# Linear attention, RMS norm and a leaky-ReLU feed-forward on one core: alternating the output's PSUM banks, holding two output products, and pinning ScalarE instructions

## The chip, the core and the metric

The kernel runs on one core of a Trainium2 chip. Its engines are TensorE (PE in the profile; PEld is its weight load), VectorE (DVE), ScalarE (ACT), GpSimd (POOL) and SyncE (SP), which work side by side and wait for each other through semaphores. TensorE writes its results to PSUM, which has banks; VectorE and ScalarE read them out ("drain" them) from there. The metric is the device time of one execution in microseconds; lower is better.

## What is computed

Eight batches of eight heads go through linear attention with an RMS norm, the result is read as 4608 tokens of width 512, and these go through a feed-forward block with 2048 hidden units. All is fp32.

```python
# q, k, v: (8, 8, 576, 64)
kv  = einsum('bhsd,bhse->bhde', k, v)
out = einsum('bhsd,bhde->bhse', q, kv)
rms = sqrt(mean(out * out, axis=-1, keepdims=True) + 1e-06)
x   = (out / rms * g_norm)            # -> transposed and reshaped to (4608, 512)
h   = x @ w_in                        # (4608, 2048)
g   = maximum(0.01 * h, h)
y   = g @ w_out                       # (4608, 512)
```

## The kernel before

The 4608 tokens are 9 blocks (NB) of 512. Block 0 is done with plain matmuls while attention and weights are still being prepared (`first_block`). Blocks 1 to 8 use Strassen's scheme: a product of 2 by 2 matrices in seven smaller products with sums around them. The hidden units are cut into four chunks (NC) per block, so a block has 4 x 7 = 28 slots. In each slot TensorE does one of the seven hidden products of a chunk (from block 2 on, two levels of Strassen) and then one of the seven output products of an earlier chunk, two slots behind (LAG).

The seven products are taken in the order 1, 2, 6, 5, 7, 3, 4. Products 1, 6, 7, 4 add up in one PSUM bank (tag 0 below) and 2, 5, 3 in the other (tag 1). Each product is read out by `done` before its bank can be written again.

```python
ORDER = (1, 2, 6, 5, 7, 3, 4)
FRESH = (1, 2, 5)

def strassen(tags, left, right, done):
    banks = {}
    for i in ORDER:
        b = tags[0 if i in (1, 6, 7, 4) else 1]
        if i in FRESH:
            banks[b] = ps_m.tile([P, 2, N2], F32, tag=b, name=f"{b[0]}_{b[1]}")   # one buffer per tag
        bank = banks[b]
        for part in range(2):
            for r in range(2):
                matmul(bank[:, part, :], lhsT=left(i, part, r), rhs=right(i, part, r), ...)
        done(i, bank.rearrange("p u (v n) -> p (u v) n", v=2))
        yield
```

The output product of chunk n (n counts chunks over the blocks 1 to 8). `to` is the sum in SBUF; only in a block's first chunk is a fresh product copied by ScalarE, everything else is a VectorE add.

```python
def product_o(n, g_sides, os, finish):
    c = n % NC
    w_sides, _ = sides_w2(n)
    sums = sides_w2(n + 1)[1] if n + 1 < NC * (NB - 1) else lambda i: None   # next chunk's weight sums by DMA
    ...
    def done(i, bank):
        key, fresh = into[i]
        to = os[key].rearrange("p u (v n) -> p (u v) n", v=2)
        if c == 0 and fresh:
            nc.scalar.copy(to, bank)
        else:
            add(nc.vector, to, bank, to)
        if c == NC - 1 and i in (2, 7, 3, 4):
            finish(key, os[key])                      # store to DRAM
        if i == 5:   sums(0)
        elif i == 4: sums(1)

    yield from strassen(("oa", "oc") if n + 1 < NC * (NB - 1) else ("hd", "hc"), ...)
```

The hidden chunk's end: sums on VectorE, four leaky ReLUs on ScalarE, four sums on GpSimd, of which output products 5, 6, 7 and 3 take s1, s2, s3 and s4.

```python
    # product_h_two, after the seven products
    add(nc.vector, g21, qa[:, :, 0, :], qa[:, :, 1, :])
    add(nc.vector, g11, qa[:, :, 0, :], qc[:, :, 0, :])
    yield
    add(nc.vector, g22, g21, qa[:, :, 2, :])
    add(nc.vector, g12, g22, qa[:, :, 3, :])
    yield
    add(nc.vector, g22, g22, qc[:, :, 1, :])
    add(nc.vector, g21, g21, qc[:, :, 1, :])
    add(nc.vector, g21, g21, qc[:, :, 2, :])
    for t in (g11, g12, g22, g21):
        relu(t)                                       # ScalarE
    sums_of(c, to):
        s1 = g21 + g22;  s2 = s1 - g11;  s3 = g11 - g21;  s4 = g12 - s2      # GpSimd
```

The division by the root mean square in `divide`, on VectorE and ScalarE by turns (the last root of a tile is one small ScalarE instruction between two VectorE ones):

```python
    for l in range(2):
        t = t2k(n, "turned")
        in_turn(nc.vector.transpose(t, sums[l]))
        in_turn(nc.vector.tensor_reduce(rms[:, l, :], t..., op=ALU.add))
        if l:
            nc.scalar.activation(rms, rms, func=AF.Sqrt, scale=1.0 / D, bias=eps_sb)
        yield
    in_turn(nc.vector.reciprocal(rms, rms))
    for l in range(2):
        nc.scalar.copy(spread..., rms[:, l, :] broadcast)
    ...
```

The last lines of block 0's loop: each hidden tile is activated by ScalarE and then multiplied by the second weight.

```python
    for n in range(2 * NC * U + 1):
        now = last
        if n < 2 * NC * U:
            ...matmuls into h_ps...
            gT = view(g_all[n // 4 % 2], n % 4 * NT, NT)
            nc.scalar.activation(gT, h_ps, func=AF.Prelu, alpha=SLOPE)
            last = (gT, w2_sb[h][c][:, u, :], n)
        ...
        for t in range(4):
            matmul(accs[t], lhsT=now[0][:, t * P:(t + 1) * P], rhs=now[1], ...)
```

The main loop, cut to what drives the output products:

```python
    for i in range(1, NB):
        ...
        for c in range(NC):
            ...
            for t in range(7):
                slot = 7 * c + t
                go(h_steps, 1)          # one hidden product
                ...                     # attention and sums for later blocks, in given slots
                if waited == LAG:
                    go_o()              # one output product
                elif o_queue:
                    waited += 1
                ...
            if i == NB - 1 and c == NC - 1:
                go(h_steps, 1)
                go_o()
            go(h_steps)
            ...
            o_queue.append(product_o((i - 1) * NC + c, g_sides, os, store(i)))
    while go_o():
        pass
```

The order of instructions on an engine is set when the program is built: a scheduler puts them in an order of its own from dependencies and its estimates of time, except where an instruction is pinned. `pin` ties an instruction behind the one that was written before it for the same engine. All matmuls are pinned, and from block 2 on (`steady`) the VectorE instructions too; most of ScalarE's are not.

Of the kernel before, what the change touches and what calls it, by code (L numbers as in the profile page):

```python
# [12 lines left out]
AF = mybir.ActivationFunctionType  # L13
# [10 lines left out]
def kernel(  # L24
# [36 lines left out]
    nc = tc.nc  # L61
    B, H, S, D = q.shape
# [8 lines left out]
    NB = B * S // NT  # L71
    N2 = NT // 2
    U = 2
    NC = DF // 2 // (U * P)
    SLOPE = 0.01
# [12 lines left out]
    ps_m = ctx.enter_context(tc.tile_pool(name="ps_m", bufs=1, space=bass.MemoryType.PSUM))  # L88

    pin = tc.keep_in_program_order  # L90
    steady = False

    def in_turn(ins):

        if steady:
            pin(ins)
# [188 lines left out]
    eps_sb = consts.tile([P, 1], F32, name="eps_sb")  # L285
# [44 lines left out]
    def x_of(lo, hi):  # L330
        return block(lo // NT)[:, :, lo % NT:lo % NT + hi - lo]
# [25 lines left out]
    def divide(lo, hi, sums):  # L357

        x, n = x_of(lo, hi), hi - lo
        rms = work.tile([P, 2, n // E], F32, tag="rms", name="rms", bufs=2)  # L360
# [3 lines that stand above are left out]
            in_turn(nc.vector.tensor_reduce(rms[:, l, :], t.rearrange("p (a i) -> p a i", i=E),  # L364
                                            axis=AX.X, op=ALU.add))
            if l:
                nc.scalar.activation(rms, rms, func=AF.Sqrt, scale=1.0 / D, bias=eps_sb)
            yield
        in_turn(nc.vector.reciprocal(rms, rms))
        spread = []  # L370
        for l in range(2):
            t = t2k(n, "spread")
            nc.scalar.copy(t.rearrange("p (a i) -> p a i", i=E),
                           rms[:, l, :].unsqueeze(2).to_broadcast([P, n // E, E]))
            spread.append(t)
        yield
        for l in range(2):
            inv = t2k(n, "inv")
            in_turn(nc.vector.transpose(inv, spread[l]))
            to = x[:, 2 * l:2 * l + 2, :]  # L380
            in_turn(nc.vector.tensor_mul(to, to, inv.unsqueeze(1).to_broadcast([P, 2, n])))
            yield
# [458 lines left out]
# [3 lines that stand above are left out]
        sums = sides_w2(n + 1)[1] if n + 1 < NC * (NB - 1) else lambda i: None  # L844
        if c == 0:
            for key in ("11", "12", "21", "22"):
                os[key] = opool.tile([P, 2, N2], F32, tag="o", name=f"o{key}", bufs=6)

        into = {1: ("11", True), 5: ("22", True), 2: ("11", False), 6: ("12", True),
                3: ("12", False), 7: ("22", False), 4: ("21", True)}  # L850
# [9 lines that stand above are left out]
                finish(key, os[key])  # L860

            if i == 5:
                sums(0)
            elif i == 4:
                sums(1)


        yield from strassen(("oa", "oc") if n + 1 < NC * (NB - 1) else ("hd", "hc"), lambda i, part, r: g_sides[i][:, 2 * r + part, :],
                            lambda i, part, r: w_sides[i][:, r, :], done)

    def go(steps, n=None):
# [13 lines left out]
    def first_block(between):  # L885

        accs = [ps_m.tile([P, DM], F32, tag=t, name="o_acc") for t in ("oa", "oc", "hb", "hd")]
        x, last = xTs.pop(0), None
# [3 lines that stand above are left out]
                c, h, u = n // (2 * U), n // U % 2, n % U  # L892
                h_ps = ps_m.tile([P, NT], F32, tag=("ha", "hc")[n % 2], name="h_ps")

                parts = 2 if n == 0 else 1
                for part in range(parts):
                    cols = slice(part * NT // parts, (part + 1) * NT // parts)
                    for e in range(NE):
                        matmul(h_ps[:, cols], lhsT=w1_sb[h][c][:, u, e, :],
                               rhs=x[:, e, cols], start=(e == 0 and part == 0),  # L900
                               stop=(e == NE - 1), skip_group_check=True)
                gT = view(g_all[n // 4 % 2], n % 4 * NT, NT)
                nc.scalar.activation(gT, h_ps, func=AF.Prelu, alpha=SLOPE)  # L903
                last = (gT, w2_sb[h][c][:, u, :], n)
            if now is None:
                continue
            between(n, 0)
            for t in range(4):
                matmul(accs[t], lhsT=now[0][:, t * P:(t + 1) * P], rhs=now[1],
                       start=(now[2] == 0), stop=(n == 2 * NC * U))  # L910
            between(n, 1)
        for t in range(4):
            o = opool.tile([P, DM], F32, tag="o", name="o", bufs=6)
            if t % 2:
                nc.scalar.copy(o, accs[t])
            else:
                nc.vector.tensor_copy(o, accs[t])
            nc.scalar.dma_start(out[t * P:(t + 1) * P, :], o)
# [8 lines left out]
    def between(n, half):  # L927
# [11 lines left out]
        if (n, half) == (12, 0):  # L939
            for p in range(2):  # L940
                load_pair(2, p)

    first_block(between)
    x_sides, _, sums, _ = sides_x(1)
    for _ in sums:
        pass
# [11 lines left out]
    LATE_SLOTS = (3, 4)  # L958

    LAG = 2  # L960
    o_queue, waited = collections.deque(), 0

    def go_o():
# [5 lines left out]
    for i in range(1, NB):  # L969
        one = i == 1  # L970
        steady = not one
        late, a_steps = a_steps, attention(i + 1, fine=not one) if i + 1 < B else iter(())
        os = {}
        for c in range(NC):
            g_sides = {}
            h_steps = product_h(c, h_sides, x_sides, g_sides) if one else \
                product_h_two(i, c, quarters, g_sides)
# [3 lines that stand above are left out]
                if not one:  # L981

                    if t == 6:
                        go(h_steps, 1)
                    if slot in LATE_SLOTS:
                        go(late, 1)
                    for _ in range(FINE_SLOTS.get(slot, 0)):
                        go(a_steps, 1)
                    if i + 1 < NB:
                        if slot == 20:  # L990
                            x_sides, new_quarters, sums, inner = sides_x(i + 1)
                        if slot in (20, 21, 22):
                            go(sums, 2 if slot == 20 else 1)
                        if slot == 24:
                            inner(0)
                        elif slot == 25:
                            inner(1)
                    load_some()
                if waited == LAG:
                    go_o()  # L1000
                elif o_queue:
                    waited += 1
                if one:

                    if t == 1:
                        combine(c, 2)
                    if t == 3 and c < NC - 1:
                        h_sides, more_h = sides_w1(c + 1)
                        combine(c + 1, 0)
                    if t == 5 and c < NC - 1:  # L1010
                        more_h()
                        combine(c + 1, 1)
                    if slot == 4:
                        go(late, 1)
                    if slot in A_SLOTS:
                        go(a_steps, 1)
                    load_some()
                    if slot == 24:
                        go(a_steps)
                        x_sides, new_quarters, sums, inner = sides_x(i + 1)  # L1020
                        go(sums)
                    elif slot == 25:
                        inner(0)
                    elif slot == 26:
                        inner(1)
# [4 lines that stand above are left out]
            if c == NC - 1 and i + 1 < NB:  # L1030
                inner(2)
                quarters = new_quarters
            if one:
                read((2, 4, RING, RING)[c])
            o_queue.append(product_o((i - 1) * NC + c, g_sides, os, store(i)))
# [32 lines left out]
```

## Time and profile before

| | before |
|---|---|
| device time, median of 3 runs | 937.8 us (937.42 to 940.43) |
| span of the profiled run | 936.3 us |
| TensorE matmul busy | 919.6 us (98%) |
| TensorE weight load busy | 776.6 us (83%) |
| VectorE busy | 618.2 us (66%) |
| ScalarE busy | 330.3 us (35%) |
| GpSimd busy | 317.9 us (34%) |
| granted TensorE clock | 0.999 |

In the lines of the profile, L118 is the helper that issues every matmul, L587 the helper that issues every sum of two tensors, L758 the leaky ReLU, L822 the copy of a hidden product by ScalarE, L856 the copy of an output product by ScalarE, L903 block 0's activation and L367 the root. `o_a` and `o_c` are the output's two banks, `h_ha` to `h_hd` the hidden products' banks; on the very last chunk the output uses `h_d` and `h_c`. A line of the timeline gives start and duration in us, engine, source line, operation, what is written from what, the shape and the count of instructions merged, and in brackets how long the engine was idle before and what it waited for.

### The profile page before, as it was taken

What the parts mean: (1) busy time and instruction counts of PE and PEld (TensorE: products, weight loads), DVE (VectorE), ACT (ScalarE), POOL (GpSimd) and SP (SyncE); (2) the same over time, 40 slices, a digit from 0 to 9 for tenths busy, and PEclk for the clock granted to TensorE, in tenths of its full rate; (3) what the DMA queues carried; (4) which work ended last, traced back from release to release, by engine and by line L of the source; (5) the groups of instructions that cost most, each with busy time, mean ns of one, the idle gap of its engine ahead of it and who ended that gap; (6) DMA issues with size and microseconds to landing.
All of it is one profiled execution on the core that took longest, in us unless ns stands there. A gap on an engine that the chain in (4) does not pass through costs nothing.

```text
span 936.3 us, 17564 instructions
## 1 busy us (share of the span) xinstructions
PE 919.6 (98%) x6856; PEld 776.6 (83%) x6856; DVE 618.2 (66%) x998; ACT 330.3 (35%) x667; POOL 317.9 (34%) x318
## 2 busy tenths in 40 slices
PE   8999999999999999999999999999999999999997
PEld 5544447888998899889988999989988999899996
DVE  4866994586457875587657865687558745654554
ACT  4544633241134332533243324332333233223321
POOL 2000364977422532235221611172225322532222
PEclk9999999999999999999999999999999999999999
DMA  8999825885697578856995589659755676567632
GB/s 270 214 242 245 249 70 186 281 285 163 214 315 231 180 238 280 257 169 199 292 281 175 168 273 302 199 168 260 232 161 173 201 218 185 173 199 220 186 110 81
DMA packets 90065, 200.02 MB, mean 214 GB/s; under 512 B 9856, under 2 KB 42112, under 8 KB 89984
## 3 DMA queue, kind: packets, MB, share of 16 engines
q1 hardware_dynamic: 79392, 186.85, 67.6%
q10 hardware_dynamic: 10144, 10.88, 3.4%
q8 instruction: 54, 0.88, 0.4%
q0 software_dynamic: 448, 1.18, 0.3%
q14 instruction: 27, 0.22, 0.1%
HBM read 172.39 MB, written 26.48 MB: 212 GB/s over the span
## 4 chain that ended last, share of the span: by engine, by line
PE 88%; DVE 7%; DMA 3%; issue 1%; ACT 1%; POOL 0%; DVEq 0%; ACTq 0%
PE o_a L118 22%; PE o_c L118 17%; PE h_ha L118 10%; PE h_hc L118 8%; PE h_hb L118 8%; PE h_hd L118 6%; PE o_acc L118 4%; PE h_ps L118 4%; PE kv_ps L118 2%; PE h_d L118 2%; PE h_a L118 2%; PE h_c L118 2%; PE h_b L118 1%; PE o_ps L118 1%; DMA stage<-in_moe_w_in_dram 1%; DVE w_all L587 1%
## 5 line engine op out<-in xcount | busy, mean ns | idle before, releaser
L587 POOL TENSOR_TENSOR gs<-g 128x512 f32<-128x512 f32 x64 | 81.3, 1289 | 447.3 <-ACT g L758 447.3
L587 DVE TENSOR_TENSOR o<-o_c,o 128x512 f32<-128x512 f32 x85 | 58.5, 688 | 108.5 <-PE o_c L118 108.4
L758 ACT ACTIVATE g<-g 128x512 f32<-128x512 f32 x124 | 78.2, 631 | 121.5 <-DVE g L587 121.5
L118 PE MATMUL o_a<-pairs,gs 128*128 128x256 f32 x496 | 117.3, 379 | 0.0
L822 ACT COPY w_all<-h_ha 128x512 f32<-128x512 f32 x84 | 48.7, 580 | 190.1 <-PE h_ha L118 190.1
L587 DVE TENSOR_TENSOR o<-o_a,o 128x512 f32<-128x512 f32 x100 | 68.7, 687 | 71.1 <-PE o_a L118 71.0
L118 PEld LDWEIGHTS o_a<-pairs,gs 128*128 128x128 f32 x496 | 90.0, 190 | 9.9
L118 PE MATMUL o_a<-w,g 128*128 128x256 f32 x248 | 59.9, 384 | 4.4 <-DVE o L587 3.8
L118 PEld LDWEIGHTS h_ha<-stage,w_all 128*128 128x128 f32 x448 | 58.8, 192 | 2.9
L118 PE MATMUL o_c<-w,g 128*128 128x256 f32 x248 | 59.7, 383 | 0.0
L118 PE MATMUL o_c<-pairs,gs 128*128 128x256 f32 x248 | 59.2, 381 | 0.0
L118 PE MATMUL o_a<-pairs,g 128*128 128x256 f32 x248 | 59.2, 381 | 0.0
L118 PE MATMUL h_ha<-stage,w_all 128*128 128x128 f32 x448 | 59.0, 275 | 0.0
L118 PE MATMUL o_acc<-w,g 128*128 128x512 f32 x128 | 58.3, 598 | 0.7 <-ACT g L903 0.7
L118 PE MATMUL o_c<-w,gs 128*128 128x256 f32 x248 | 58.7, 379 | 0.0
L118 PE MATMUL h_ps<-xT,w_all 128*128 128x512 f32 (+1 forms) x136 | 58.0, 570 | 0.2 <-DVE w_all L255 0.2
L587 DVE TENSOR_TENSOR g<-g,pairs 128x512 f32<-128x512 f32 x84 | 55.6, 689 | 1.9
L118 PEld LDWEIGHTS o_a<-w,g 128*128 128x128 f32 x248 | 44.9, 190 | 13.5 <-DVE o L587 7.5
L587 POOL TENSOR_TENSOR pairs<-w_all 128x512 f32<-128x512 f32 x8 | 11.1, 1388 | 124.3 <-ACT cut L244 105.5
L118 PEld LDWEIGHTS o_c<-w,g 128*128 128x128 f32 x248 | 44.9, 190 | 8.4 <-issue 3.1
L118 PEld LDWEIGHTS o_c<-pairs,gs 128*128 128x128 f32 x248 | 44.9, 190 | 6.5 <-issue 1.4
L118 PEld LDWEIGHTS o_a<-pairs,g 128*128 128x128 f32 x248 | 44.9, 190 | 6.5 <-DVE w_all L587 0.9
(203 smaller groups left out, 1982.5 us busy)
## 6 DMA issues: line engine op xcount, KB each, us to landing
w_all<-w SPq DMA_DIRECT2D x196, 448.0 KB, 4.2
pairs<-w SPq DMA_DIRECT2D x56, 512.0 KB, 4.5
out_dram<-o ACTq DMA_DIRECT2D x36, 256.0 KB, 4.3
v_in<-in_v_dram SPq DMA_DIRECT2D x29, 288.0 KB, 6.0
k_in<-in_k_dram SPq DMA_DIRECT2D x28, 288.0 KB, 6.3
q_in<-in_q_dram SPq DMA_DIRECT2D x56, 144.0 KB, 6.6
q_in<-in_q_dram SPq DMA_DIRECT2D x56, 140.0 KB, 6.5
w<-stage SPq DMA_DIRECT2D x12, 512.0 KB, 4.3
```

The lines of the kernel that those rows point to most:

```text
L118: pin(nc.tensor.matmul(*args, **kw))
L587: ins = eng.tensor_tensor(out_, a, b_, op=ALU.subtract if minus else ALU.add)
L758: nc.scalar.activation(t, t if src is None else src, func=AF.Prelu, alpha=SLOPE)
L822: nc.scalar.copy(q[:, at], banks[tag])
```

## The change

Three things are changed.

First, the two output banks change roles with every chunk: in an even chunk products 1, 6, 7, 4 go to `oa` and 2, 5, 3 to `oc`, in an odd chunk the other way round. Before, every chunk began and ended on `oa`, so the last product of a chunk and the first of the next were in one bank. The last chunk's use of two of the hidden products' banks goes away. Second, in the last block two slots (22 and 25) run without an output product, so that two more of them are left for the time after the last hidden product, when the last chunk's sums are still being made. Third, two kinds of ScalarE instruction are pinned to their written order: the last activation of block 0, and every root written after block 0.

```diff
-    steady = False
+    steady = first_done = False
...
             if l:
-                nc.scalar.activation(rms, rms, func=AF.Sqrt, scale=1.0 / D, bias=eps_sb)
+                act = nc.scalar.activation(rms, rms, func=AF.Sqrt, scale=1.0 / D, bias=eps_sb)
+                if first_done:
+                    pin(act)
...
-        yield from strassen(("oa", "oc") if n + 1 < NC * (NB - 1) else ("hd", "hc"), lambda i, part, r: g_sides[i][:, 2 * r + part, :],
+        yield from strassen((("oa", "oc"), ("oc", "oa"))[n % 2], lambda i, part, r: g_sides[i][:, 2 * r + part, :],
                             lambda i, part, r: w_sides[i][:, r, :], done)
...
                 gT = view(g_all[n // 4 % 2], n % 4 * NT, NT)
-                nc.scalar.activation(gT, h_ps, func=AF.Prelu, alpha=SLOPE)
+                act = nc.scalar.activation(gT, h_ps, func=AF.Prelu, alpha=SLOPE)
+                if n == 2 * NC * U - 1:
+                    pin(act)
...
     first_block(between)
+    first_done = True
...
     LAG = 2
+
+
+    HELD = (22, 25)
...
-                if waited == LAG:
+                if slot in HELD and i == NB - 1:
+                    pass
+                elif waited == LAG:
                     go_o()
```

## The prediction, made before the changed kernel was run

> **What bounds the kernel now.** I read the page first, for the engines and the granted clock, then the waits of TensorE and of its weight load, then the timeline around each wait that the change touches.
>
> ```profile
> PE 919.6 (98%) x6856; PEld 776.6 (83%) x6856; DVE 618.2 (66%) x998; ACT 330.3 (35%) x667; POOL 317.9 (34%) x318
> PE 88%; DVE 7%; DMA 3%; issue 1%; ACT 1%; POOL 0%; DVEq 0%; ACTq 0%
> ```
>
> TensorE is busy 98% of the span, the chain that ended last runs through it for 88%, and the clock was granted at 0.999. The change takes no matmul away, so it can win only what TensorE idles: 936.3 - 919.6 = 16.7 us in all, part of it the start and the last store. Which instructions those idle times stand before is in the waits:
>
> ```profile
> PE o_a L118 <- DVE o L587: 3.8, 6, 1.3
> PE h_d L118 <- POOL gs L587: 2.3, 1, 2.3
> PE o_acc L118 <- ACT g L903: 0.7, 1, 0.7
> PE o_a L118 <- ACT o L856: 0.6, 1, 0.6
> PEld o_a L118 <- DVE o L587: 7.5, 6, 1.5
> ```
>
> Columns: total us, times, longest. The weight load's 7.5 us is the same six waits seen earlier in the pipe. It overlaps a matmul, so the matmul's start times say what was lost. In the undisturbed stretch from block 2 a slot is regular: `h_ha` or `h_hc` takes 0.89 us from start to start, `h_hb` or `h_hd` 0.67, an output product 1.73, together 3.29. I listed every piece that is longer than that after 140 us, and found only eight: seven before an `o_a` that begins a chunk, one at the end.
>
> **What the skill says.** The Trainium skill, "PSUM — Partial Sum Buffer", section "PSUM bank collisions raise a hardware error", asks that PSUM be guarded by bank and quadrant, not by address. A fresh product in `oa` therefore waits until the last product in `oa` has been read, and one in `oc` doesn't. The trace agrees: all seven stalls are at `o_a` after `o_a`, none at `o_c`. "Perfetto Trace Analysis", section "Matmuls", advises rotating independent groups through banks; that is part one of the change. The PSUM page's section "Engine vs sequencer instructions" calls the queues of ScalarE, VectorE and GpSimd strict FIFO: an instruction that waits holds up all behind it. The trace agrees, see block 0 below.
>
> **Part one, the banks.** The longest of the seven, in order of time:
>
> ```profile
> 802.05 1.89 PE L118 MATMUL o_a<-pairs,g 128*128 128x256 f32 x8
> 803.47 0.68 DVE L587 TENSOR_TENSOR w_all<-h_hc,w_all 128x512 f32<-128x512 f32 x1
> 804.07 0.55 DVE L587 TENSOR_TENSOR pairs<-h_hd,pairs 128x384 f32<-128x384 f32 x1
> 804.53 1.60 DVE L587 TENSOR_TENSOR xt<-xT,xt 128x512 f32<-128x512 f32 x1
> 806.06 0.68 DVE L587 TENSOR_TENSOR o<-o_a,o 128x512 f32<-128x512 f32 x1
> 806.79 1.99 PE L118 MATMUL o_a<-w,g 128*128 128x256 f32 x8 [1.29 <-DVE o L587]
> ```
>
> The product ended near 803.94. Its drain needs 0.68 us but stands in VectorE's queue behind two hidden drains and a sum for the next block, and finishes at 806.74. TensorE had only one hidden product between (1.56 us) and was ready for the next `o_a` at 804.67 + 0.67 = 805.34: 1.45 us lost. With the banks swapped, the product at 805.34 goes to the other bank, whose last product ended a slot earlier and was drained at 803.55 (its sum began at 802.87 and took 0.68). The first bank is needed one whole slot later, at 805.34 + 3.29 = 808.63, against a drain at 806.74: 1.89 us of slack at the worst place. As four chunks are an even number, roles alternate across blocks too.
>
> The seven, from start times: at 316, 415, 514, 612 and 712 us the gap between a small attention product and the `o_a` after it is 0.71, 0.62, 0.49, 0.39 and 0.28, where it normally overlaps by 0.07, so 0.78 + 0.69 + 0.56 + 0.46 + 0.35 = 2.84. At 686 it is 0.73 (a ScalarE copy of `o_a` queued behind a root, the fourth line of the waits), at 805 it is 1.45. After each of these two the product is also 0.1 longer to the next start. Sum: 2.84 + 0.83 + 1.55 = 5.2 us.
>
> **Part two, the two held products.**
>
> ```profile
> 911.51 0.83 PE L118 MATMUL h_hb<-stage,w_all 128*128 128x128 f32 x6
> 918.64 0.68 DVE L587 TENSOR_TENSOR o<-o_a,o 128x512 f32<-128x512 f32 x1
> 918.76 0.63 ACT L758 ACTIVATE g<-g 128x512 f32<-128x512 f32 x1 [0.70 <-DVE g L587]
> 919.46 2.49 POOL L587 TENSOR_TENSOR gs<-g 128x512 f32<-128x512 f32 x2 [18.43 <-ACT g L758]
> 921.91 1.27 POOL L587 TENSOR_TENSOR gs<-gs,g 128x512 f32<-128x512 f32 x1
> 923.23 1.99 PE L118 MATMUL h_d<-pairs,gs 128*128 128x256 f32 x8 [2.25 <-POOL gs L587]
> ```
>
> The last hidden product is followed by an output product at 912.18. From there the chain VectorE, ScalarE, three GpSimd sums (s1, s3, s2 in that order) takes 923.23 - 912.18 = 11.05 us until product 6 of the last chunk can start. TensorE has five products to do meanwhile, 5 x 1.73 = 8.65, so it stands still for 2.4, and refills for another 0.1. Held back, two more products make 7 x 1.73 = 12.1 us, more than 11.05: the wait goes away. No work is added; the hidden products end 2 x 1.73 = 3.46 us earlier.
>
> One small wait comes in its place. The end now uses only `oa` and `oc`. Counted from the output product after the last hidden one, the third product ends near 5.35, but its drain is written behind three sums of g and ended, in the trace before, at 918.64 + 0.68 - 912.18 = 7.14. The fifth is in the same bank and would start at 4 x 1.73 = 6.92; I give it 0.25 plus 0.1 of refill. Net: 2.5 - 0.35 = 2.15 us. The weight sums of the last chunk, which SyncE reloads after products 5 and 4 of the chunk before, landed in 3.6 to 6.0 us here. The first is issued about 3.6 us into this stretch and needed at 12.1, the second at about 9.4 and needed near 16: neither becomes the bound.
>
> **Part three, the pins.**
>
> ```profile
> 137.53 3.60 PE L118 MATMUL o_acc<-w,g 128*128 128x512 f32 x8
> 140.25 0.30 ACT L367 ACTIVATE rms<-rms,eps_sb 128x8 f32<-128x8 f32 x1 [8.04 <-DVE rms L364]
> 140.82 0.49 ACT L373 COPY spread<-rms 128x128 f32<-128x128 f32 x2 [0.27 <-DVE rms L369]
> 141.23 0.59 ACT L903 ACTIVATE g<-h_ps 128x512 f32<-128x512 f32 x1
> 141.87 3.70 PE L118 MATMUL o_acc<-w,g 128*128 128x512 f32 x8 [0.74 <-ACT g L903]
> ```
>
> The last hidden tile of block 0 was ready by about 137.7. Its activation came at 141.23, because a root was ordered ahead of it and kept ScalarE waiting 8.04 us. In the written order this root belongs to block 1's fifth slot, about 20 us later. With both pins the activation runs when its tile is ready, and the two products take 2 x 3.43 = 6.86 from start to start instead of 7.87: 1.0 us. The other pinned roots free ScalarE's queue (it waited 44.5 us for roots, in 14 waits), but the only TensorE wait from it is the 0.6 at 686, already counted.
>
> **The sum.** 5.2 + 2.15 + 1.0 = 8.35 us off 937.8: 929.4. For small waits that a new order of the unpinned instructions may bring, I leave 0.3: **929.7 us**, 0.9% faster.
>
> **Rivals.** (a) *VectorE is the real limit at a chunk's start, and the wait only moves to the chunk's second product.* For it: VectorE's queue was 2.1 us late at 806. Against: the slack of 1.89 us there, and a mean load of 66%. It would leave 2 to 4 of the 5.2: 931.5 to 933.5. (b) *The end keeps its wait*, because the held products' drains push the g sums back on VectorE, or because a hidden bank isn't drained in time when slots 22 and 23 have no product between them. For it: in slot 21 ScalarE's second copy ended at 896.25, and with 1.73 us less the bank would be wanted near 896.6, only 0.4 later. It would leave 0 to 1 of the 2.15: 931 to 932. (c) *The pins hurt:* a root fixed behind a hidden copy delays the reciprocal, VectorE is in order too, and drains come late; or an unpinned ScalarE or GpSimd order comes out worse. For it: the scheduler sees different times. Against: a root's consumers are slots away. A few us: 932 to 938, past 940 only if a stall repeats in each block.
>
> **Range and chances.** Below: every listed stall with no replacement, and a run at the low edge of 937.42, would give about 927.5. Above: (a) and (b) together give some 934. So 927.5 to 934.0. Faster by over 2% needs 18.8 us, more than TensorE's whole idle time: 0.01. Slower by over 2% needs a repeated new stall: 0.02. Within 2%: 0.97.
>
> **What would show it.** TensorE's waits no longer list `o_a` for VectorE (or a total under 0.5 us); matmul busy stays near 919 us, so all of the gain is idle time. Near 137 us the activation comes before the root and the two `o_acc` follow each other at 3.43. At the end product 6 follows its predecessor without a GpSimd wait, with a wait of about 0.3 us for VectorE three products earlier. I am wrong if new waits of TensorE for `o_c` or a hidden bank appear, or if the start before 100 us, which nothing here should touch, moves by a microsecond.

## Result and profile after

The changed kernel takes 931.57 us (median of 4 runs, 930.64 to 932.72) against 937.61 us before (4 runs, 936.59 to 940.43): a ratio of 0.9931, 95% interval 0.9905 to 0.9957. Measured again beside other kernels on another chip it had 930.44 us (5 runs) against 940.03 us (9 runs), ratio 0.991, interval 0.9894 to 0.9927. It is faster by 0.7% to 0.9%, far inside 2%.

The page's engine line and chain of the changed kernel; the columns are busy time, share of the span and instructions:

```profile
PE 918.4 (99%) x6856; PEld 776.2 (84%) x6856; DVE 619.2 (67%) x998; ACT 331.0 (36%) x667; POOL 319.0 (34%) x318
PE 95%; DMA 2%; DVE 2%; issue 0%; ACT 0%; POOL 0%; ACTq 0%; DVEq 0%; POOLq 0%
```

No engine has fewer instructions: TensorE's busy time fell by 1.2 us, VectorE's rose by 1.0. The span fell by 7.3 us (936.3 to 929.0). TensorE's share of the chain rose from 88% to 95%, VectorE's fell from 7% to 2%. These shares name the engines on the chain; how much was won is read from the waits and the stretches below.

After the start-up the list of TensorE's waits in the changed kernel has one that the kernel before did not have (total us, times, longest):

```profile
PE h_b L118 <- ACT g L785: 0.5, 1, 0.5
```

All four waits of TensorE that the prediction listed are gone: `o_a` for VectorE, `o_a` for ScalarE, `h_d` for GpSimd, `o_acc` for ScalarE. The new one stands before a hidden bank, `h_b`, and is for ScalarE. New waits before a hidden bank were among the signs by which the prediction said it would be wrong; the size of this one is below.

I divided both runs at the same five places: the first hidden product of block 0, the first of block 1, the first of block 2, the first of block 8, and the end of the last matmul. The columns are the stretch, its length, and busy time with the count of instructions for PE, PEld, DVE, ACT and POOL, then clock, DMA share and GB/s. First before, then after:

```profile
26.87:145.40 118.53, 117.62 (x508) 52.81 (x505) 97.65 (x173) 54.07 (x111) 21.45 (x16) 1.00 0.81 200
145.40:232.98 87.58, 87.58 (x585) 74.13 (x584) 54.00 (x90) 27.84 (x55) 68.07 (x68) 1.00 0.73 237
232.98:821.79 588.81, 584.46 (x4738) 535.43 (x4737) 395.54 (x615) 204.69 (x418) 197.24 (x201) 1.00 0.73 221
821.79:932.13 110.34, 108.09 (x689) 99.73 (x687) 58.14 (x91) 30.60 (x56) 26.01 (x21) 1.00 0.53 159
```

```profile
26.78:144.30 117.52, 117.35 (x508) 52.89 (x505) 96.23 (x168) 53.35 (x108) 21.43 (x16) 1.00 0.86 206
144.30:232.33 88.03, 87.58 (x585) 73.87 (x584) 56.37 (x95) 28.31 (x58) 68.22 (x68) 1.00 0.72 234
232.33:815.90 583.57, 583.57 (x4738) 535.29 (x4736) 395.61 (x615) 205.51 (x418) 198.11 (x201) 1.00 0.73 223
815.90:924.12 108.22, 108.09 (x689) 99.75 (x687) 58.14 (x91) 30.61 (x56) 26.05 (x21) 1.00 0.53 162
```

Length minus the first busy figure is TensorE's idle time. In blocks 2 to 7 it was 4.35 us and is 0.00; block 8 with the end goes from 2.25 to 0.13; block 0 from 0.91 to 0.17; block 1 from 0.00 to 0.45. From the first hidden product to the last matmul the kernel takes 905.26 us before and 897.34 after, 7.92 less.

The place of the longest stall, in the changed kernel (block 7's last chunk boundary; start, duration, engine, instruction):

```profile
797.72 1.89 PE L118 MATMUL o_c<-pairs,g 128*128 128x256 f32 x8
799.13 0.68 DVE L589 TENSOR_TENSOR w_all<-h_hc,w_all 128x512 f32<-128x512 f32 x1
799.73 0.55 DVE L589 TENSOR_TENSOR pairs<-h_hd,pairs 128x384 f32<-128x384 f32 x1
800.20 1.61 DVE L589 TENSOR_TENSOR xt<-xT,xt 128x512 f32<-128x512 f32 x1
801.01 1.89 PE L118 MATMUL o_a<-w,g 128*128 128x256 f32 x8
801.73 0.68 DVE L589 TENSOR_TENSOR o<-o_c,o 128x512 f32<-128x512 f32 x1
804.30 1.89 PE L118 MATMUL o_c<-w,g 128*128 128x256 f32 x8
```

VectorE's queue is as before, and the drain of the last product is as late as before: it starts 4.01 us after that product (801.73 - 797.72), as it did at 806.06 - 802.05. But the next product now starts 3.29 us after the last one, in the other bank. The drained bank is wanted again at 804.30 and is free at 802.41: 1.89 us of slack. Nothing got faster; what was late no longer matters.

The end, in the changed kernel:

```profile
906.29 1.89 PE L118 MATMUL o_a<-pairs,gs 128*128 128x256 f32 x8
908.02 1.89 PE L118 MATMUL o_c<-w,gs 128*128 128x256 f32 x8
909.30 0.68 DVE L589 TENSOR_TENSOR o<-o_a,o 128x512 f32<-128x512 f32 x1
910.04 1.99 PE L118 MATMUL o_a<-pairs,g 128*128 128x256 f32 x8
912.58 1.27 POOL L589 TENSOR_TENSOR gs<-gs,g 128x512 f32<-128x512 f32 x1
915.32 1.89 PE L118 MATMUL o_c<-pairs,gs 128*128 128x256 f32 x8
```

The GpSimd sum that product 6 needs is done at 913.85, and product 6 comes at 915.32 without waiting. The small new wait is there too: the product at 910.04 would have followed at 909.75, but its bank was drained only at 909.98.

Block 0's last activation, in the changed kernel:

```profile
137.44 7.03 PE L118 MATMUL o_acc<-w,g 128*128 128x512 f32 x16
137.64 0.60 ACT L905 ACTIVATE g<-h_ps 128x512 f32<-128x512 f32 x1 [5.53 <-PE h_ps L118]
155.88 0.28 ACT L367 ACTIVATE rms<-rms,eps_sb 128x8 f32<-128x8 f32 x1
```

The activation runs as soon as its tile is there, at 137.64 (141.23 before), and the two output sums follow each other without a wait. The root now comes at 155.88, in block 1.

### The profile page after: what moved, and what is told of

It is laid out like the page before. It is cut to its first block, busy times and chain, and to the rows that moved or that the text cites. A ratio compares the mean times of both kernels' runs of the same rounds, so it can differ in the third digit from the quotient of the medians.

```text
span 929.0 us, 17587 instructions
## 1 busy us (share of the span) xinstructions
PE 918.4 (99%) x6856; PEld 776.2 (84%) x6856; DVE 619.2 (67%) x998; ACT 331.0 (36%) x667; POOL 319.0 (34%) x318
## 4 chain that ended last, share of the span: by engine, by line
PE 95%; DMA 2%; DVE 2%; issue 0%; ACT 0%; POOL 0%; ACTq 0%; DVEq 0%; POOLq 0%
PE o_a L118 21%; PE o_c L118 21%; PE h_ha L118 11%; PE h_hb L118 8%; PE h_hc L118 8%; PE h_hd L118 6%; PE o_acc L118 6%; PE h_ps L118 6%; PE o_ps L118 2%; PE kv_ps L118 2%; PE h_a L118 1%; PE h_b L118 1%; DMA pairs<-in_v_dram 1%; PE h_c L118 1%; PE h_d L118 1%; DMA pairs<-in_moe_w_out_dram 1%
## 5 line engine op out<-in xcount | busy, mean ns | idle before, releaser
L589 DVE TENSOR_TENSOR o<-o_c,o 128x512 f32<-128x512 f32 x104 | 71.6, 689 | 111.8 <-PE o_c L118 111.8
L589 DVE TENSOR_TENSOR o<-o_a,o 128x512 f32<-128x512 f32 x88 | 60.5, 687 | 68.0 <-PE o_a L118 67.9
L118 PE MATMUL o_c<-pairs,gs 128*128 128x256 f32 x384 | 91.3, 381 | 0.0
L118 PE MATMUL o_a<-pairs,gs 128*128 128x256 f32 x384 | 90.8, 379 | 0.0
L118 PEld LDWEIGHTS o_c<-pairs,gs 128*128 128x128 f32 x384 | 69.8, 190 | 9.3 <-issue 1.4
L118 PEld LDWEIGHTS o_a<-pairs,gs 128*128 128x128 f32 x384 | 69.8, 190 | 7.8
L118 PE MATMUL o_c<-w,g 128*128 128x256 f32 x256 | 61.6, 383 | 0.0
L118 PEld LDWEIGHTS h_ps<-xT,w_all 128*128 128x128 f32 x136 | 25.5, 190 | 29.2 <-issue 26.5
L589 DVE TENSOR_TENSOR g<-w_all 128x512 f32<-128x512 f32 x28 | 21.8, 780 | 40.9 <-ACT w_all L824 40.9
L589 DVE TENSOR_TENSOR w_all<-h_hc,w_all 128x512 f32<-128x512 f32 x56 | 38.4, 686 | 15.3 <-PE h_hc L118 15.0
```

What stands on the lines that cost most here:

```text
L118: pin(nc.tensor.matmul(*args, **kw))
L589: ins = eng.tensor_tensor(out_, a, b_, op=ALU.subtract if minus else ALU.add)
```

## Experiments

I use the lengths of the stretches from the traces, in us: block 0, block 1, blocks 2 to 7, block 8 with the end, and their sum.

| kernel | block 0 | block 1 | blocks 2-7 | block 8, end | sum | ratio of times to before on the same chip (interval) |
|---|---|---|---|---|---|---|
| before | 118.53 | 87.58 | 588.81 | 110.34 | 905.26 | 1 |
| changed | 117.52 | 88.03 | 583.57 | 108.22 | 897.34 | 0.9931 (0.9905 to 0.9957) |
| banks only | 118.54 | 87.34 | 583.57 | 110.33 | 899.78 | 0.9934 (0.9911 to 0.9956) |
| held only | 118.55 | 87.98 | 588.83 | 108.22 | 903.58 | 0.9987 (0.9970 to 1.0005) |
| pins only | 117.74 | 88.36 | 587.97 | 110.33 | 904.40 | 0.9980 (0.9965 to 0.9995) |
| changed, one held | 117.52 | 88.02 | 583.57 | 108.61 | 897.72 | 0.9915 (0.9898 to 0.9932) |
| before, a sum doubled | 118.54 | 87.34 | 606.83 | 112.02 | 924.73 | one run |
| changed, a sum doubled | 117.53 | 88.01 | 583.57 | 108.22 | 897.33 | one run |
| changed, no root pins | 118.54 | 87.50 | 583.57 | 108.22 | 897.83 | one run |
| changed, two repairs | 117.51 | 87.54 | 583.69 | 107.83 | 896.57 | 0.9889 (0.9872 to 0.9906) |
| changed, again | 117.52 | 88.03 | 583.56 | 108.22 | 897.33 | 0.9910 (0.9894 to 0.9927) |
| two repairs, again | 117.52 | 87.56 | 583.57 | 107.82 | 896.47 | 0.9919 (0.9904 to 0.9935) |

The expectations below call the third stretch "blocks 2 to 8"; it ends where block 8 begins.

**Each part alone.** The banks alone:

```diff
-        yield from strassen(("oa", "oc") if n + 1 < NC * (NB - 1) else ("hd", "hc"), ...
+        yield from strassen((("oa", "oc"), ("oc", "oa"))[n % 2], ...
```

> The kernel before with the alternating banks alone (nothing held, nothing pinned). My theory: the seven stalls before a chunk's first output product are bank waits, and with the swap TensorE gains a whole slot (3.29 us), so all 5.2 us go: the span falls from 936.3 to about 931.1, the time to about 932.4; the 2.3 us wait for GpSimd at the end and the 0.7 us wait for block 0's last activation stay. Rival (VectorE is the limit at a chunk's start, the wait moves to the chunk's second product): TensorE gets new waits of 2 to 4 us in all before the other output bank, the span stays at 933.5 to 935.

Blocks 2 to 7 take 583.57 us, the changed kernel's figure, 5.24 less than before. The trace has no wait for VectorE before either output bank. Block 0 (118.54) and the end (110.33) are as before, with these two waits:

```profile
PE o_c L118 <- POOL gs L587: 1.8, 1, 1.8
PE o_acc L118 <- ACT g L903: 0.7, 1, 0.7
```

So the banks give 5.2 of the gain, and the stall did not move to the second product. The wait for GpSimd is 1.8 and not 2.25 only because the product before it had already come 0.38 late, behind a leaky ReLU; the end is no shorter.

The two held products alone:

```diff
+    HELD = (22, 25)
...
-                if waited == LAG:
+                if slot in HELD and i == NB - 1:
+                    pass
+                elif waited == LAG:
```

> The kernel before with the two held output products alone. My theory: the end's wait for GpSimd (2.25 us, and 0.1 of refill) goes, a wait of about 0.3 us for VectorE comes before the fifth product of the end: 2.1 us less, span about 934.2, time 935.5; the bank stalls stay at 5.2 us. Rival (the held products' drains only push the last sums back): the wait for GpSimd stays at 1 us or more and the span at 935.3 or above.

Block 8 with the end takes 108.22 us, 2.12 less, with no wait for GpSimd and 0.28 before the fifth product. The rival's wait did not come. The time doesn't show it: block 1 happened to take 0.40 more here, and the first hidden product came at 29.16 us instead of 26.87 (see the last section), so the span was 936.9, which lies where the rival had put it, for another reason. The interval of the ratio includes 1.

The pins alone:

```diff
-                nc.scalar.activation(rms, rms, func=AF.Sqrt, scale=1.0 / D, bias=eps_sb)
+                act = nc.scalar.activation(rms, rms, func=AF.Sqrt, scale=1.0 / D, bias=eps_sb)
+                if first_done:
+                    pin(act)
...
+                if n == 2 * NC * U - 1:
+                    pin(act)
```

> The kernel before with the pins alone. My theory: block 0's two last output sums follow each other without a wait (1.0 us less), block 1 gets a new wait of 0.45 us before a hidden bank, because the root's division now falls into block 1 (as in the changed kernel's trace near 161 us), and the stall of 0.83 us near 686 us, where a copy stood behind a root, goes; the other six bank stalls stay. Sum: 1.4 us less, span about 934.9. Rival (pins matter in every block): a change of 3 us or more in either direction.

Blocks 2 to 7 lose 0.84 us: the stall near 686 us is gone, the other six stay. Block 0 is 0.79 shorter, block 1 0.78 longer. The first is 0.2 less and the second 0.3 more than I gave; in the sum 0.86 less in place of 1.4. In the kernels whose roots are not pinned, block 1 varies between 87.34 and 87.98, so of its 0.78 I trust only that it is longer.

The three parts alone give 5.48 + 1.68 + 0.86 = 8.02; together they gave 7.92. They overlap in the stall near 686 us (0.83, cured by the banks and by the pins alike), which the spread of block 1 hides in the sum.

**How many to hold.**

```diff
-    HELD = (22, 25)
+    HELD = (25,)
```

> The changed kernel with one product held (slot 25) and not two. My theory: the last chunk's sums need 11.05 us after the last hidden product, six products fill 10.4 of it, seven 12.1; so with one held TensorE waits again for GpSimd, about 0.4 to 0.7 us, and the kernel ends 0.4 us later than the changed one (span near 929.4 where that had 929.0). Rival (holding only frees VectorE at slots 22 and 25, the count doesn't matter): no GpSimd wait and the same end.

The end comes 0.39 us later (108.61 against 108.22), as worked out; the span, 931.7, shows more because the first hidden product came at 29.86 us here. How it comes about was only half foreseen:

```profile
912.82 1.89 PE L118 MATMUL o_a<-pairs,g 128*128 128x256 f32 x8
914.21 0.63 ACT L760 ACTIVATE g<-g 128x512 f32<-128x512 f32 x1 [0.70 <-DVE g L589]
914.92 1.97 PE L118 MATMUL o_c<-w,g 128*128 128x256 f32 x8 [0.22 <-ACT g L760]
917.36 1.26 POOL L589 TENSOR_TENSOR gs<-gs,g 128x512 f32<-128x512 f32 x1
918.68 0.48 PE L118 MATMUL o_c<-pairs,gs 128*128 128x256 f32 x1
```

Two waits share the loss. Before the last chunk's first product TensorE stood for the leaky ReLU, 0.37 longer than the usual 1.73 from start to start; before product 6 it stood for the GpSimd sum, 0.22 longer. The profile puts the first down to the ReLU, which ended at 914.84; but the drain of that product's bank, written behind the three sums of g, ended at 914.77 in this trace, so the late drain that I had foreseen would have held it almost as long. Together with the restarts they come to what one wait for GpSimd would have cost, because both hang on the same chain: product 6 starts 918.68 - 907.63 = 11.05 us after the output product that follows the last hidden one, exactly as in the kernel before. That chain has its own length whatever TensorE does meanwhile. The second held product takes the waits away; one alone leaves them.

**Slack at the chunk's start.** In both kernels, a sum for the next block is written twice in the blocks 2 to 7, so that VectorE's queue is longer by one instruction ahead of the late drain; the output is the same.

```diff
+        def again():                       # beside the sums of the next block
+            add(nc.vector, t4, b21, t2, True)
...
                         if slot in (20, 21, 22):
                             go(sums, 2 if slot == 20 else 1)
+                        if slot == 22:
+                            again()
```

> The kernel before, with the last sum for the next block (slot 22, blocks 2 to 7) done twice; the result is unchanged, VectorE has one more sum of 0.7 to 0.8 us in its queue ahead of the drain of the chunk's last output product. My theory (in the kernel before TensorE waits there for VectorE's place in the queue, with no slack): each of the six stalls grows by the whole 0.7 to 0.8 us, 4.2 to 4.8 us in all; the stretch of blocks 2 to 8, 588.8 us before, becomes 593.0 to 593.6. Rival (VectorE has room at that point): no change.

> The changed kernel with the same sum done twice. My theory: the swap left 1.89 us of slack at the worst place, so 0.7 to 0.8 us more costs nothing: TensorE still has no wait for VectorE before an output bank, the stretch of blocks 2 to 8 stays at 583.6 us. Rival (VectorE is the limit and the swap only just covers it): waits before the other output bank, 1 to 4 us.

In the kernel before, the direction was right and the size far too small. Blocks 2 to 7 grew by 18.02 us, to 606.83, and the run took 957.45 us beside a median of 940.2. The wait, over the same six stalls:

```profile
PE o_a L118 <- DVE o L587: 13.8, 6, 3.0
```

It was 3.8 and is 13.8: 10.0 us over six stalls, 1.67 each. I had given the sum 0.7 to 0.8 us. It takes 1.61 (the prediction's own lines have 1.60 at 804.53), and twice 3.27:

```profile
414.52 3.27 DVE L587 TENSOR_TENSOR xt<-xT,xt 128x512 f32<-128x512 f32 x2
```

So the dose was 1.66, and TensorE paid all of it. "SBUF — State Buffer", section "Who interferes with whom", of the Trainium skill says that a VectorE instruction with two SBUF inputs contends with GpSimd's reads of SBUF. The trace fits: the same kind of sum takes 0.69 us at 407.59 us in this trace, with GpSimd idle, and here GpSimd's sums run at the same time. An estimate from these figures: in the kernel before, a sum of 0.68 us here would have let each drain begin 0.93 us earlier, and five of the seven stalls were shorter than that (0.35 to 0.78 us). By this estimate the sums on GpSimd have a part in VectorE's lateness; moving them was not tried.

The remaining 8 us are not waits. The windows of this run at the end of the second of the six stalls and after it (the last three columns are clock, DMA share and GB/s):

```profile
418.00:420.00 2.00, 1.55 (x5) 1.34 (x6) 1.67 (x3) 0.00 (x0) 0.92 (x1) 0.80 0.44 178
420.00:422.00 2.00, 2.00 (x8) 1.69 (x7) 0.44 (x1) 0.00 (x0) 0.00 (x0) 0.50 0.00 0
422.00:424.00 2.00, 2.00 (x15) 1.95 (x15) 1.16 (x3) 0.88 (x2) 1.14 (x2) 0.85 0.00 0
```

After a stall of 2.27 us TensorE's granted clock went down to 0.50 for 3.41 us (419.20 to 422.61), and the product there took 3.08 us instead of 1.99. This followed five of the six stalls and also the wait of 2.25 us at the end, so that block 8 with the end took 112.02 us in place of 110.34 (see the last section).

In the changed kernel the same dose cost nothing: 583.57 us, and no wait of TensorE for VectorE there. The place with the least slack:

```profile
802.05 3.29 DVE L589 TENSOR_TENSOR xt<-xT,xt 128x512 f32<-128x512 f32 x2
802.87 1.89 PE L118 MATMUL o_a<-w,g 128*128 128x256 f32 x8
805.26 0.68 DVE L589 TENSOR_TENSOR o<-o_c,o 128x512 f32<-128x512 f32 x1
```

The bank is free at 805.94 and wanted at 802.87 + 3.29 = 806.16. Of 1.89 us of slack 0.22 is left, which is 1.89 less the dose. A dose of one sum hence nearly filled it, so the swap covers today's queue but not any queue: by this reckoning, with more than another 0.22 us VectorE would become the limit there.

**The pins on the roots.**

```diff
                 act = nc.scalar.activation(rms, rms, func=AF.Sqrt, scale=1.0 / D, bias=eps_sb)
-                if first_done:
-                    pin(act)
```

> The changed kernel without the pins on the roots (the activation's own pin stays). My theory: the root again goes ahead of block 0's last activation, which costs 1.0 us in block 0 (118.5 us from its first hidden product to block 1's, where the changed kernel has 117.5), and block 1 loses its new wait (87.3 to 87.6 us in place of 88.0); blocks 2 to 8 stay at 583.6 us, as the pinned roots there gate no output product once the banks alternate. In all 0.3 to 0.6 us slower than the changed kernel from the first hidden product on. Rival (the pins of the later roots carry part of the gain): blocks 2 to 8 get longer by half a microsecond or more.

Block 0 takes 118.54 again, block 1 87.50, blocks 2 to 7 stay at 583.57: 0.49 us slower in sum. The root stands ahead of the last activation and waits 8.04 us, although that activation keeps its own pin:

```profile
140.18 0.30 ACT L367 ACTIVATE rms<-rms,eps_sb 128x8 f32<-128x8 f32 x1 [8.04 <-DVE rms L364]
141.15 0.59 ACT L903 ACTIVATE g<-h_ps 128x512 f32<-128x512 f32 x1
141.80 1.55 PE L118 MATMUL o_acc<-w,g 128*128 128x512 f32 x3 [0.75 <-ACT g L903]
```

A pin ties an instruction behind the one written before it; it doesn't keep a later one from being put ahead. So the pin on the activation does nothing by itself, and the pins on the roots are worth something in block 0 alone once the banks alternate. Whether they would do without the activation's pin was not run.

**Repairing the two new waits.** The root's division goes from slot 4 of block 1 to slot 12, where VectorE was busy only 0.69 of 3.5 us; and the third drain of the end is written before the last of the sums of g.

```diff
-                    if slot == 4:
+                    if slot == 12:
                         go(late, 1)
...
         add(nc.vector, g21, g21, qc[:, :, 1, :])
+        yield
         add(nc.vector, g21, g21, qc[:, :, 2, :])
...
                 go(h_steps, 1)
                 go_o()
+                go(h_steps, 1)
+                go_o()
             go(h_steps)
```

> The changed kernel with its two new waits repaired: block 1 does the pinned root's division in slot 12 and not in slot 4, and at the end the third drain is written before the last of the sums of g. My theory: the 0.6 us wait for ScalarE before the hidden bank in block 1 goes (block 1 near 87.4 us), the 0.3 us before the end's fifth product goes and the sums still arrive before product 6 needs them (11.05 + 0.7 = 11.75 us against 12.1), so from the first hidden product to the last matmul it takes 0.8 to 1.0 us less than the changed kernel (897.3 there), 896.4. The time is 930.7 where the changed kernel has 931.6, a difference within the spread of the runs. Rival (a wait moved is a wait kept): a new wait of 0.3 us or more in block 1 or before product 6.

> The changed kernel once more, beside the repaired one on the same chip. The kernel's own stretch, from the first hidden product to the last matmul, is 897.3 us again (905.3 before); the times of single runs spread by about 2 us with the length of the stage ahead of it (26 to 30 us), so a median 7 to 8 us below the kernel before, with a run-to-run range of 2 us.

> The kernel with the two repairs beside the changed one. Theory: its stretch is 896.6 us, 0.8 less than the changed kernel's, and the median is lower by 0.5 to 1 us, which the spread of the start may hide. Rival (the lower time of its first measurement was the chip's): equal medians within 0.3 us, or the order reversed.

In the traces both waits are gone: block 1 takes 87.54 and 87.56, the end 107.83 and 107.82, and the sum is 0.77 and 0.86 us below the changed kernel's. In the times it can't be told: beside each other on one chip the repaired kernel had 931.12 us (929.69 to 933.12) and the changed one 930.44 (929.6 to 933.04). The lower ratio of its first measurement, 0.9889, did not come back: of the medians the rival was right, the order is reversed. By the measured times it does not beat the changed kernel. The changed kernel itself was 9.59 us below the kernel before this time, more than the 7 to 8 expected.

## Why the prediction was right

Predicted were 929.7 us and a range of 927.5 to 934.0; measured 931.57, and 930.44 the second time. The parts of the sum hold one by one:

- **Banks, 5.2 us.** Measured 5.24 in blocks 2 to 7, with the banks alone and together with the rest. That all seven stalls are a wait for one bank is shown by the banks alone, which take all seven away; that 1.89 us of slack would be left is shown by the trace and by the doubled sum. Rival (a), that the wait moves to the second product, did not happen.
- **Held products, 2.15 us.** Measured 2.12. The new wait, put at 0.25 plus 0.1 of refill, was 0.29 plus 0.1. With one held, the end is 0.39 later, which the length of the chain (11.05 us) gives.
- **Block 0, 1.0 us.** Measured 1.01. The pins on the roots are needed for it; the activation's own pin, of which I had expected a part, does nothing without them.
- **What the sum left out: block 1, 0.45 us.** I wrote that the pinned root "belongs to block 1's fifth slot", and that a root's consumers are slots away, and stopped there. I did not ask what the division that hangs on it would collide with. VectorE's work moved from 141 to 143 us, where GpSimd was idle, into 156 to 160, beside GpSimd's sums. Its two products with `inv` took 1.47 and 1.15 us there in place of 0.43 and 0.42, and the division held up a hidden drain, behind that a leaky ReLU, behind that the copy of `h_b`:

```profile
156.43 0.50 ACT L375 COPY spread<-rms 128x128 f32<-128x128 f32 x2 [0.27 <-DVE rms L371]
157.10 1.47 DVE L383 TENSOR_TENSOR xT<-xT,inv 128x256 f32<-128x256 f32 x1
158.83 1.15 DVE L383 TENSOR_TENSOR xT<-xT,inv 128x256 f32<-128x256 f32 x1
159.90 0.68 DVE L589 TENSOR_TENSOR g<-h_c,g 128x512 f32<-128x512 f32 x1
160.61 0.63 ACT L760 ACTIVATE g<-g 128x512 f32<-128x512 f32 x1 [2.02 <-DVE g L589]
161.15 0.57 ACT L785 COPY g<-h_b 128x512 f32<-128x512 f32 x1
161.86 1.32 PE L118 MATMUL h_b<-xt,pairs 128*128 128x256 f32 x5 [0.45 <-ACT g L785]
```

The product `h_c` was done by 156.23 but drained at 159.90; in the kernel before, with the division done earlier, the product ended at 157.33 and its drain began at 157.37. That is rival (c) in small: 0.45 us once, not in each block. Moving the division to another slot removes the wait, so the division at this place is its cause. How much of it is the new place in VectorE's queue and how much the slower products beside GpSimd was not separated; the products lost 1.77 us, more than the wait. My 0.3 us of allowance was for new orders of unpinned instructions; that it nearly covered this is luck.

The sum is then 5.24 + 2.12 + 1.01 - 0.45 = 7.92 us, the difference of the two traces from the first hidden product on. Of this TensorE's idle time makes 6.76 and shorter busy time (fewer restarts) 1.15.

How near a median comes to 929.7 is in part chance. The medians differ by 6.04 us in the first comparison and 9.59 in the second; single runs are spread by the start, where the first hidden product came up to 3.65 us later in one trace than in another (last section). So a start that moves by a microsecond, which the prediction took for a sign of being wrong, would have told nothing. The range's lower end also doesn't follow from its own terms: 937.42 less 5.2, 2.5 and 1.0 is 928.7 and not 927.5. Neither end was reached.

## What to carry to other kernels

Two products in a row in one PSUM bank give the reader of the first only the time between them, and an in-order reader may be late for reasons of its own; let the roles of two banks alternate so that the same bank never comes twice in a row, and the same lateness costs nothing as long as it is under the slot that is won (here 3.29 us; with stalls of up to 3.0 us, by the doubled sum, it held). Fill a chain of fixed length at the end with work held back from the steady part: count the products that its length asks for. When pinning moves an instruction, follow the work that hangs on it to its new place and look at what runs there.

## What I had not expected of the hardware

**The spread between runs is made before 30 us.** The first hidden product starts at 26.21 to 29.86 us in these twelve traces, while blocks 2 to 7 repeat to a hundredth (583.56 to 583.57 us in the six traces with alternating banks and without a repair). In the middle of some 60 small attention products that wait for nothing the profile shows, TensorE stands for 1.0 to 3.0 us ("issue"). The longest, in the waits of the kernel with one product held:

```profile
PE o_ps L118 <- issue: 3.0, 1, 3.0
```

The windows of the same run:

```profile
17.00:19.00 2.00, 0.00 (x0) 0.00 (x0) 0.43 (x1) 0.92 (x2) 0.00 (x0) 1.00 0.94 295
19.00:21.00 2.00, 1.60 (x37) 0.85 (x36) 0.29 (x1) 0.93 (x2) 0.00 (x0) 0.82 1.15 205
21.00:23.00 2.00, 2.00 (x11) 0.77 (x10) 1.97 (x6) 0.76 (x2) 0.00 (x0) 0.50 1.05 267
23.00:25.00 2.00, 1.91 (x10) 0.96 (x7) 0.43 (x1) 0.95 (x2) 0.00 (x0) 0.82 1.07 213
```

Where this stop was 2.2, 2.7 or 3.0 us (three traces) the clock then fell to 0.50 for 3.41 us, and the first hidden product came at 28.65 to 29.86. Where it was 1.0 to 2.0 us (nine traces) it came at 26.21 to 27.23. The whole spread of 3.65 us is near what the stop (1.04 to 2.99) and half of 3.41 us explain: 1.95 + 1.7. Each run's record has its mean clock, and one such fall lowers it by 0.002 over 930 us. In the second comparison the changed kernel's two runs at 0.998 took 932.71 and 933.04 us, the other three 929.60 to 930.44; of the kernel before, the five at 0.998 took 940.03 to 941.09, the other four 937.95 to 939.85. Like with like, the medians differ by 7.6 and 8.4 us, near the 7.92 of the traces.

Why TensorE stops there is not settled, but the traces have a trail. In each of the twelve, one 16 KB packet of the DMA queue that the page lists as `instruction` (q8) is moved at that time, and the stop ends 1.4 to 1.7 us after this packet does, whether the packet ends at 15.82 us (stop until 17.23) or at 17.75 (until 19.40). That TensorE waits there for its instructions is thus likely. It is no proof: some 50 later packets of this queue go with no such stop, and no run moved the packet. The DMA engines are fully busy at that time (share 0.94 to 1.15); whether that delays the packet was not tried.

**A short stop can cost twice, and where it falls decides.** "TensorE: Matmul & The Clock Gate" of the Trainium skill, section "HAM oscillation", warns of idle gaps above some 3.4 us. Here shorter ones were enough. The traces record the granted clock with the times of its changes. While matmuls ran it fell nine times in the twelve traces, each time to 0.50 and for 3.41 us: in three starts, after five of the six lengthened stalls, and after the wait at the end of that same run. All changes of a trace lie whole multiples of 3.41 us after its first rise (at 4.67 to 6.64 us); four falls of the run with the long stalls, at 419.20, 521.60, 624.00 and 726.40, are 102.40 us apart, 30 times 3.413.

So I divided each trace into windows of 3.41 us, counted from its first rise. In the nine windows just before a fall TensorE's matmuls were idle for 57% to 80% of the time (1.96 to 2.71 us). In no other whole window up to the last matmul were they idle for more than 55% (1.89 us), and the clock never fell after one of these. The length of a stop alone does not decide, as one and the same stop of 2.25 us shows, the wait for GpSimd at the end. The first line is a window of the kernel before, the others are two of that kernel with the doubled sum:

```profile
921.34:924.75 3.41, 1.52 (x7) 1.37 (x8) 0.37 (x1) 0.00 (x0) 3.10 (x3) 1.00 0.22 77
938.03:941.44 3.41, 1.16 (x6) 0.99 (x6) 0.69 (x1) 0.00 (x0) 3.33 (x3) 1.00 0.22 77
941.44:944.85 3.41, 3.41 (x10) 2.70 (x9) 0.69 (x1) 0.00 (x0) 0.20 (x1) 0.50 0.00 0
```

In the kernel before a border between two windows divides the stop, 1.89 us of it lie in this one, and the clock stays at 1.00. With the doubled sum all 2.25 us lie in one window, the next runs at 0.50, and the end is 1.68 us longer. In these runs a stop of TensorE under 1.9 us was never paid for again; a longer one was, by up to half of 3.41 us, when enough of it fell into one window. Where the windows lie changes from run to run. Between 1.89 and 1.96 us nothing was measured, and stops of other kinds were not tried.
